# The MLP behind attention in program order, in parts of four and six chunks, with six chunks beside attention instead of seven

## The chip, the cores and the metric

The kernel runs on one core of one Trainium2 chip. The time is the device time of one execution in microseconds (us). The kernel before takes 1400.59 us, the median of three runs (1400.41 to 1401.59). One execution was also taken by the hardware profiler; its span, from the first to the last instruction, is 1397.3 us.

The names of the engines are those of the profile: PE multiplies matrices (TensorE; PEld is its loading of weights), DVE is VectorE, ACT is ScalarE, POOL is GpSimd, and SP issues most of the transfers (DMAs). Each engine works off its own queue in the order in which the instructions stand there. What one engine needs of another it waits for at a semaphore, and all that stands behind the waiting instruction on that engine waits too.

## What is computed

Masked attention over 8 batches of 8 heads (576 positions of 64 numbers), and behind it an MLP with one hidden layer of 2048 over the 4608 rows that attention leaves. q, k, v are float32; `w_in` and `w_out` come as float64.

```python
def attention(q, k, v, tau):                      # (8, 8, 576, 64)
    scores = q @ k.transpose(0, 1, 3, 2) / sqrt(64)
    top = scores.max(-1, keepdims=True)
    scores = where(scores >= top - tau, scores, -1e9)
    a = exp(scores - top)
    return (a / (a.sum(-1, keepdims=True) + 1e-9)) @ v

def mlp(x, w_in, w_out, alpha):                   # x: (4608, 512)
    h = x @ w_in                                  # (512, 2048)
    g = maximum(h, 0) + alpha * minimum(h, 0)
    return g @ w_out                              # (2048, 512)
```

## The kernel before

**Numbers in two parts.** Every operand of the MLP is held as a high and a low part, and a product is three matmuls: high by high, high by low, low by high. The hidden layer is cut into 16 chunks of 128. For one chunk and one group of tokens, layer 1 is 4 blocks of the 512 inputs by 3 products, 12 matmuls into a tile `ph`; layer 2 is 3 matmuls for each 128 tokens, added up over the chunks in a tile `acc`.

**Attention.** Two heads make a pair, and there are 32 pairs, each of nine units (128 queries by one head). The loop over `i` goes through the units in cycles. In each, PE does the scores `s` of one unit and the transposes `t` of another, DVE takes the row maximum (`nmx`, L410), masks (L430) and makes low parts, and ACT does the exponentials and the high parts. The last step of a pair multiplies by v (`av`), turns the reciprocals of the sums (`rp`, L565), fetches them back spread over the partitions (`rb`), and writes a part of x to memory (`fin_mul` L589, `fin_out` L595). The order in which these instructions stand is that in which the code emits them (`manual_schedule`).

**MLP, part 1, beside attention.** The first F1 = 7 chunks are done for groups of G1 = 256 tokens as soon as the x of a group is there, with names that end in "a" (`pha`, `pta`, `ga`, `acca`). There are 18 groups, 0 to 17. `Mlp.cycle` gives out the steps: it has a budget of PE time per cycle (CYCLE) less what attention uses there; a layer 1 step costs 1.31 of it and a layer 2 matmul 0.216. GB buffers hold the `ga`. The sums over the 7 chunks go through `po` to a buffer `part` in memory.

**Decoding.** `Split64` makes the two parts of a float64 weight out of its bits, for one chunk of w_in or w_out (a piece): a load of 512 KB; `size`, two ACT instructions; four steps on DVE and partly POOL (`clamp`, `shift`, `sign`, `power`); `round` on ACT, which makes the high part; `rest`, two steps; and `join` on POOL, which makes the low part and is the last reader of the loaded words. 14 pieces for the 7 chunks are decoded in the first cycles.

**Behind attention.** What is left of part 1 is written by `drain`, outside the manual schedule: there the scheduler of the tool that builds the program orders the instructions by its own estimate of times. The 18 pieces of the other nine chunks are decoded there too, with two buffers `w0` for the loaded words. In this place layer 1's result goes through `hidden`: two DVE instructions (L872, L873), a copy on ACT for the high part and a subtraction on POOL for the low part (both in `split_g`).

**MLP, part 2.** The other nine chunks for nine groups of G2 = 512 tokens, with names that end in "b" (`phb`, `ptb`, `gb`, `accb`): per group nine layer 1 steps, then four blocks of 128 tokens with 27 matmuls each. A block is added to its row of `part` (`pin`, a load) on DVE (`ob`, L903) and stored. The x of a group is loaded at once (`load_x`) and split at once (`split_x`: one ACT copy for `xh`, one POOL subtraction for `xl`).

Of the kernel before, what the change touches and what calls it, by code (L numbers as in the profile page):

```python
# [35 lines left out]
GB = 11  # L36
ENG1 = ('vpp', 'vpp')
ENG2 = ('vvp', 'vvv')
TAIL = 4
# [30 lines left out]
def tile_masked_attention_moe(  # L70
# [31 lines left out]
    class Split64:  # L102
        """float64 bits -> hi + lo in float32r, to 24 bits or better."""
# [105 lines left out]

    def prelu2(t, r, n):  # L210
        nc.gpsimd.tensor_tensor(t[:, :n], t[:, :n], r[:, :n], op=ALU.add)
# [32 lines left out]
    class Turned:  # L244
        """The transposed scores of two heads, in parts, with columns of ones that sum v."""
# [21 lines left out]
    class Pair:  # L267
        """The steps of two heads of one batch; each queues work on one or two engines."""
# [8 lines left out]
        def load(self, what):  # L277
# [11 lines left out]
            if pi == 0:  # L289
                # The first pair's are doubled on the way in, so that its scores start at once.  # L290
# [20 lines left out]
        def prep_first(self, j):  # L311
            """The splits of q and k for one head, before there is other work."""
# [11 lines left out]
        # The two heads' q and k come one above the other. The parts are made so, and then moved:  # L324
        # qst holds the parts of q one above the other, kh and kl each part of k twice.
# [51 lines left out]
        # A unit is (chunk of queries, head), or the tail: the last queries of the  # L377
        # first head above the first queries of the second.
# [63 lines left out]
        def turn_k(self, u):  # L442
            """The keys beyond the four blocks: of both heads at once for a chunk of queries."""
# [13 lines left out]
        def places(self, u):  # L457
            """(PSUM, its place in SBUF by part) for the unit's transposed blocks."""
# [98 lines left out]
        # Divide by the sums; rows that kept no score get the mean of v.  # L557
# [49 lines left out]
    # Where in a pair's nine cycles the work beside the softmax falls.  # L607
# [39 lines left out]
    class Mlp:  # L647
        """The part of the MLP that runs beside attention, a little in each cycle."""
# [15 lines left out]
        def step_l1(self, i):  # L664
# [10 lines left out]

            def act(ph=ph):
                st[fi] = prelu1(mem.mp1, G1, fcs1[fi], n, ph, name, 2)
                prelu2(*st[fi], n)

            def spl():  # L680
                g = mem.mp1.tile([P, 2, G1], F32R, tag="g", name=f"g{name}", bufs=GB)
                split_g(g, st.pop(fi)[0], n, dict(p=nc.gpsimd, v=nc.vector).get(SPG))
                st["g"][fi] = g
# [29 lines left out]
        def cycle(self, i, used, slot):  # L713
            """Work for the tensor engine up to the cycle's length."""
# [12 lines left out]

        def drain(self):
            """What is left when attention is done, in the scheduler's order."""
            for gi, st, fi in list(self.l1):  # L730
                t0, n = groups1[gi]
                if fi is None:
                    pool = (mem.mp1, wp2)[gi % 2]
                    xr = load_x(pool, t0, n, G1, 1)
                    st["x"] = split_x(pool, xr, t0, n, G1, 1)
                else:
                    st["g"][fi] = hidden(mem.mp1, ps_2, G1, fcs1[fi], n, st["x"], f"a{gi}_{fi}", GB)
                if fi == F1 - 1:
                    for o in range(0, n, P):
                        self.l2.extend((0, gi, st, o, fj, ti) for fj in range(F1) for ti in range(3))  # L740
                if not self.l2 or fi != F1 - 1:
                    continue
                while self.l2:
                    _, gj, sj, o, fj, ti = self.l2.popleft()
                    nj = groups1[gj][1]
                    m = min(P, nj - o)
                    if fj == 0 and ti == 0:
                        self.acc = ps_2.tile([P, 512], F32, tag="acc", name=f"acca{gj}_{o}", bufs=4)
                    layer2(self.acc, fcs1[fj], sj["g"][fj], o, m, fj == 0, fj == F1 - 1, (ti,))
                    if fj == F1 - 1 and ti == 2:  # L750
                        po = mem.mp1.tile([P, DM], F32, tag="po", name=f"po{gj}_{o}", bufs=1)
                        nc.scalar.activation(po[:m], self.acc[:m], AF.Copy)
                        nc.sync.dma_start(part[gj][o : o + m, :], po[:m])
                decode_some(4)
            self.l1.clear()
# [14 lines left out]
    # The words of a piece of w_in wait where w_out's parts will be; those of w_out  # L770
    # in the place of its next chunk.
# [6 lines left out]
    for n_, (w, fc, io) in enumerate(pieces):  # L778
        c = DEC0 + DEC * n_ if n_ < F1 else DECO0 + DECO * (n_ - F1)
        if n_:  # L780
            at_cycle(max(-3, c - LD) if io == "i" else c - 3, w.load)
# [62 lines left out]
    for i in sorted({*soon, *later}):  # L844
        for fn, a in soon.get(i, []) + later.get(i, []):
            fn(*a)
# [110 lines left out]
```

## Time and profile before

| | |
|---|---|
| device time, median of 3 runs | 1400.59 us |
| span of the profiled execution | 1397.3 us |
| busy PE / DVE / ACT / POOL | 1339.4 / 975.7 / 820.9 / 762.3 us |
| last row maximum of attention starts | 818.16 us |
| first matmul of part 2 starts | 947.71 us |
| last matmul ends | 1393.5 us |
| mean granted clock of PE | 0.995 |

The time is about 3.3 us above the span. The execution has three stages: attention with part 1 beside it until 818 us; the rest of part 1, with 18 pieces decoded, until 948 us; part 2. Busy time counts matmuls that overlap in the pipeline as one stretch, so a PE that is busy all the time may still have work at less than its best pace. The best pace of a matmul is read from a long row of them without a wait. A line of the trace begins with the start and the length in us; a "x" at its end counts instructions of the row.

### The profile page before, as it was taken

What the parts mean: (1) busy time and instruction counts of PE and PEld (TensorE: products, weight loads), DVE (VectorE), ACT (ScalarE), POOL (GpSimd) and SP (SyncE); (2) the same over time, 40 slices, a digit from 0 to 9 for tenths busy, and PEclk for the clock granted to TensorE, in tenths of its full rate; (3) what the DMA queues carried; (4) which work ended last, traced back from release to release, by engine and by line L of the source; (5) the groups of instructions that cost most, each with busy time, mean ns of one, the idle gap of its engine ahead of it and who ended that gap; (6) DMA issues with size and microseconds to landing.
All of it is one profiled execution on the core that took longest, in us unless ns stands there. A gap on an engine that the chain in (4) does not pass through costs nothing.

```text
span 1397.3 us, 23301 instructions
## 1 busy us (share of the span) xinstructions
PE 1339.4 (96%) x8116; PEld 1181.2 (85%) x8116; DVE 975.7 (70%) x1933; ACT 820.9 (59%) x1843; POOL 762.3 (55%) x821
## 2 busy tenths in 40 slices
PE   5888899999999999999999999888999999999998
PEld 4556789999999999999999998777888888888887
DVE  6999988888888898898888957986323323323332
ACT  7788888888888888888888854453112012111100
POOL 3776676666676666576676557566434124223311
PEclk9999999999999999999999999999999999999999
DMA  8643634545545444454454214433320220111011
GB/s 249 184 127 106 180 105 122 162 116 142 147 117 150 139 134 131 132 154 127 128 160 132 83 57 153 132 109 128 121 74 17 91 91 33 59 61 42 19 61 38
DMA packets 94628, 157.67 MB, mean 113 GB/s; under 512 B 14160, under 2 KB 39024, under 8 KB 94512
## 3 DMA queue, kind: packets, MB, share of 16 engines
q1 hardware_dynamic: 94512, 156.19, 38.4%
q8 instruction: 65, 1.06, 0.3%
q14 instruction: 51, 0.42, 0.1%
HBM read 85.53 MB, written 28.46 MB: 82 GB/s over the span
## 4 chain that ended last, share of the span: by engine, by line
PE 80%; DVE 9%; ACT 4%; DMA 2%; issue 2%; POOL 2%; SPq 0%; DVEq 0%; POOLq 0%; ACTq 0%
PE phb L194 16%; PE accb L224 16%; PE s L395 10%; PE av L542 10%; PE acca L224 9%; PE pha L194 9%; PE t L439 7%; DVE p L430 2%; DVE nmx L410 2%; DMA wri<-in_moe_w_in_dram 1%; PE tk L455 1%; DVE wti L135 1%; POOL wi L152 1%; ACT xb L555 1%; ACT xa L553 1%
## 5 line engine op out<-in xcount | busy, mean ns | idle before, releaser
L410 DVE TENSOR_REDUCE nmx<-s 128x1 f32<-128x576 f32 x288 | 217.0, 753 | 72.6 <-PE s L395 69.5
L215 ACT ACTIVATE gb<-ptb 128x512 fp32r<-128x512 f32 x81 | 50.9, 630 | 337.7 <-DVE ptb L873 337.3
L218 POOL TENSOR_TENSOR gb<-ptb,gb 128x512 fp32r<-128x512 f32 x81 | 104.4, 1290 | 257.0 <-ACT gb L215 256.8
L224 PE MATMUL acca<-wo,ga 128*128 128x512 f32 x756 | 230.7, 419 | 7.2 <-ACT ga L215 4.0
L224 PE MATMUL accb<-wo,gb 128*128 128x512 f32 x972 | 221.9, 389 | 0.0
L224 PEld LDWEIGHTS accb<-wo,gb 128*128 128x128 f32 x972 | 182.4, 188 | 37.9
L430 DVE SCALAR_TENSOR_TENSOR p<-s,thr,p 128x576 f32<-128x576 f32 x256 | 206.6, 807 | 1.3 <-ACT thr L423 0.9
L194 PE MATMUL phb<-xh,wi 128*128 128x512 f32 x648 | 202.9, 392 | 1.1 <-ACT xh L180 1.1
L194 PE MATMUL pha<-xh,wi 128*128 128x256 f32 x1008 | 199.7, 284 | 3.7 <-DVE pta L873 3.4
L418 ACT ACTIVATE p<-s,nmx 128x576 f32<-128x576 f32 x256 | 190.0, 742 | 10.8 <-DVE nmx L410 10.5
L395 PE MATMUL s<-kh,qst 128*128 128x288 f32 x640 | 142.2, 312 | 38.1 <-DVE p L430 23.3
L194 PEld LDWEIGHTS pha<-xh,wi 128*128 128x128 f32 x1008 | 163.8, 190 | 9.9 <-DVE pta L873 4.6
L224 PEld LDWEIGHTS acca<-wo,ga 128*128 128x128 f32 x756 | 132.8, 191 | 28.6 <-ACT ga L215 5.3
L439 PE MATMUL t<-ident,p 128*128 128x128 f32 x1024 | 154.6, 274 | 0.0
L395 PEld LDWEIGHTS s<-kh,qst 128*128 128x128 f32 x640 | 101.4, 193 | 61.5 <-issue 29.4
L903 DVE TENSOR_TENSOR ob<-accb,pin 128x512 f32<-128x512 f32 x36 | 24.2, 689 | 181.9 <-PE accb L224 181.9
L194 PEld LDWEIGHTS phb<-xh,wi 128*128 128x128 f32 x648 | 122.6, 189 | 27.2 <-ACT xh L180 1.5
L194 PE MATMUL pha<-xl,wi 128*128 128x256 f32 x504 | 142.2, 282 | 0.0
L872 DVE TENSOR_SCALAR ptb<-phb,alpha_sb 128x512 f32<-128x512 f32 x81 | 60.7, 751 | 108.5 <-PE phb L194 96.4
L395 PE MATMUL s<-kl,qst 128*128 128x288 f32 x640 | 133.8, 299 | 0.0
L194 PE MATMUL phb<-xl,wi 128*128 128x512 f32 x324 | 127.2, 393 | 3.6 <-POOL xl L182 3.6
L439 PEld LDWEIGHTS t<-ident,p 128*128 128x128 f32 x1024 | 126.5, 141 | 0.1
(117 smaller groups left out, 2772.6 us busy)
## 6 DMA issues: line engine op xcount, KB each, us to landing
kr<-in_k_dram SPq DMA_DIRECT2D x31, 320.0 KB
rb<-rvd SPq DMA_DIRECT2D x64, 144.0 KB
xs<-xa SPq DMA_DIRECT2D x32, 288.0 KB
part<-po SPq DMA_DIRECT2D x36, 256.0 KB
pin<-part SPq DMA_DIRECT2D x36, 256.0 KB
out_dram<-ob SPq DMA_DIRECT2D x36, 256.0 KB
vr<-in_v_dram SPq DMA_DIRECT2D x28, 320.0 KB
qr<-in_q_dram SPq DMA_DIRECT2D x31, 288.0 KB
```

The costliest lines, as they stand in the source:

```text
L194: nc.tensor.matmul(ph[:, :n], w[:, c, :], xx[:, c, :n], start=(c == 0 and ti == 0), stop=(c == NCC - 1 and ti == 2),)
L215: nc.scalar.activation(g[:, 0, :n], t[:, :n], AF.Copy)
L218: nc.gpsimd.tensor_tensor(g[:, 1, :n], t[:, :n], f(g[:, 0, :n]), op=ALU.subtract)
L224: nc.tensor.matmul(acc[:m, :], gg[:, g, o : o + m], w, start=(first and ti == 0), stop=(last and ti == 2))
L395: nc.tensor.matmul(ps[:, h, :288], w, kk[:, a + h * 288 : a + (h + 1) * 288], start=(ki == 0 and i == 0), stop=(ki == 1 and i == n - 1),)
L410: nc.vector.tensor_reduce(self.nmx[:, j : j + 1], self.S[u][0][:, :, :288], axis=AX.XY, op=ALU.max, negate=True)
L418: nc.scalar.activation(pj, ps[:, :, :288], AF.Exp, bias=nmx[:, j : j + 1], scale=1.0)
L430: nc.vector.scalar_tensor_tensor(pj, ps[:, :, :288], thr[:, j : j + 1], pj, op0=ALU.is_ge, op1=ALU.mult, accum_out=self.sm[:, c : c + 1])
L439: nc.tensor.transpose(tb[:, c, :], pt[:, j, j * D + c * P : j * D + (c + 1) * P], ident)
L542: nc.tensor.matmul(pa[:m, :n], w, x, start=(part == 0 and c == 0), stop=(part == z.parts[-1] and c == NKC))
L872: nc.vector.tensor_scalar(t[:, :n], ph[:, :n], 0.0, alpha_sb[:, fc : fc + 1], op0=ALU.min, op1=ALU.mult)
L903: nc.vector.tensor_tensor(ob[:m], acc[:m], pi_[:m], op=ALU.add)
```

## The change

- F1 goes from 7 to 6 and GB from 11 to 10: 12 pieces instead of 14 are decoded early, part 1 has six chunks, and part 2 has ten.
- `drain`, `decode_some` and `hidden` are gone. The loop over `i` now runs on in the manual schedule until part 1 is done, with the whole budget for the MLP once attention is over (`used = 0.0`). A layer 1 step there takes `prelu` (two DVE instructions) and an ACT copy, as `hidden` did.
- Part 2 goes twice over the nine groups: chunks 6 to 9 first, whose sums are added to `part` and written back there, then chunks 10 to 15, whose sums go to the output.
- The eight pieces of chunks 6 to 9 are decoded in the cycles behind attention, one every two cycles (DEC2 = 4, halved); those of chunks 10 to 15 one every five cycles during the first pass of part 2 (a cycle there is a layer 1 step or a block). There are three buffers `w0` instead of two.
- x is fetched for part 2 in four pieces per group (`fetch_x`), each split for itself two cycles later; `pin` is loaded by cycle.

The core of the diff:

```diff
-F1 = 7
+F1 = 6
-GB = 11
+GB = 10
-TAIL = 4
+CLOSE = 9
+DEC2, DEC3 = 4, 5
...
+            alone = i >= total
+
             def act(ph=ph):
+                if alone:
+                    st[fi] = (prelu(mem.mp1, G1, fcs1[fi], n, ph, name, 2),)
+                    return
...
-        def drain(self):
...
+    parts2 = [fcs2[:4], fcs2[4:]]
...
+    def decode_part(part, c0, step):
+        for n_, (io, fc) in enumerate((io, fc) for io in "io" for fc in part):
+            w = Split64(mem.wp2, ("w0", 3), mem.wp2, ("w1", 3), ENG2[(fc + (io == "o")) % 2], *(src_i if io == "i" else src_o)(fc))
+            c = c0 + step * n_ // 2
+            decode_at(c, mem.wp2, w, fc, io, c - 2)
...
+            if i > total + CLOSE and not (mlp.l1 or mlp.l2 or nready < len(groups1)):
+                break
...
+            if i == total + CLOSE:
+                at.close()
+                mem.wp2 = wp2_.enter_context(tc.tile_pool(name="wp2", bufs=1, reuse_waits="tile"))
+                decode_part(parts2[0], i + 3, DEC2)
+                first = fetch_x(mem.wp2, *groups2[0], i + 4, "0_0")
...
+            if i >= total:
+                used = 0.0
...
+        decode_part(parts2[1], i + 3, 2 * DEC3)
+        for num, (p, k) in enumerate(todo):
+            fcs, (t0, n), st = parts2[p], groups2[k], nxt
...
+            for fc in fcs:
+                ph = ps_2.tile([P, 512], F32, tag="ph", name=f"phb{p}{t0}_{fc}", bufs=4)
+                while "x" not in st:
+                    cycle()
+                layer1_into(ph, fc, n, st["x"])
+                cycle()
+                t = prelu(mp2, G2, fc, n, ph, f"b{p}{t0}_{fc}", 2)
...
+                split_g(gg, t, n)
+                g.append(gg)
+            for o, m in blocks:
...
+                for j, fc in enumerate(fcs):
+                    layer2(acc, fc, g[j], o, m, j == 0, j == len(fcs) - 1)
+                cycle()
...
+                dst = out[t0 + o : t0 + o + m, :] if p == len(parts2) - 1 else part[gi][r : r + m, :]
+                nc.sync.dma_start(dst, ob[:m])
```

How the order of the instructions changes is shown at three places. In the names, `wi8` and `wo8` are the two parts of chunk 8's weights, `wti8` and `wri8` their working tile and loaded words, and `ga15_2` is the split hidden layer of group 15, chunk 2; the number behind the last underscore tells buffers apart.

The first is ACT behind attention, where group 14 of the kernel before is done. L123 and L124 are `size`, which waits for the load of its piece, L144 is `round`, L215 the high part of `ga`:

```order
L215 ACTIVATE ga14_1_12391<-pta14_1_12388 128x256
L123 ACTIVATE wti8_12324<-wri8_12322 128x512
L124 ACTIVATE wri8_12322<-wri8_12322 128x512
L215 ACTIVATE ga14_2_12410<-pta14_2_12407 128x256
L123 ACTIVATE wto8_12338<-wro8_12336 128x512
L124 ACTIVATE wro8_12336<-wro8_12336 128x512
L215 ACTIVATE ga14_3_12429<-pta14_3_12426 128x256
L144 ACTIVATE wi8_12331<-wti8_12324 128x512
L215 ACTIVATE ga14_4_12448<-pta14_4_12445 128x256
```

The same engine in the changed kernel, one group later (the lines are now L124, L125, L145 and L222; L720 is `po`):

```order
L145 ACTIVATE wi7_12103<-wti7_12009 128x512
L124 ACTIVATE wti9_12106<-wri9_12060 128x512
L125 ACTIVATE wri9_12060<-wri9_12060 128x512
L808 ACTIVATE xh0_0_12024<-xr0_0_3_12064 128x512
L222 ACTIVATE ga15_0_12139<-pta15_0_12113 128x256
L145 ACTIVATE wi8_12163<-wti8_12057 128x512
L124 ACTIVATE wto6_12166<-wro6_12109 128x512
L125 ACTIVATE wro6_12109<-wro6_12109 128x512
L222 ACTIVATE ga15_1_12171<-pta15_1_12142 128x256
L720 ACTIVATE po14_128_12190<-acca14_128_12069 128x512
L222 ACTIVATE ga15_2_12197<-pta15_2_12174 128x256
```

In both, a `size` stands ahead of copies of `ga`; in the changed kernel the pieces come as four of w_in and then four of w_out, each `size` two cycles behind the last, and parts of x for part 2 stand among them.

The second place is POOL in the changed kernel over the same stretch; L153 is `join`, L225 the low part of `ga`, L150 half of `rest`, L809 a part of `xl`:

```order
L153 TENSOR_TENSOR wi6_12054<-wti6_11959,wri6_11916 128x512
L809 TENSOR_TENSOR xl0_0_12025<-xr0_0_3_12064,xh0_0_12024 128x512
L225 TENSOR_TENSOR ga15_0_12139<-pta15_0_12113,ga15_0_12139 128x256
L153 TENSOR_TENSOR wi7_12103<-wti7_12009,wri7_11962 128x512
L225 TENSOR_TENSOR ga15_1_12171<-pta15_1_12142,ga15_1_12171 128x256
L150 TENSOR_TENSOR wti8_12057<-wti8_12057,wi8_12163 128x512
L225 TENSOR_TENSOR ga15_2_12197<-pta15_2_12174,ga15_2_12197 128x256
L153 TENSOR_TENSOR wi8_12163<-wti8_12057,wri8_12012 128x512
```

Before, the same engine had this there:

```order
L152 TENSOR_TENSOR wo8_12345<-wto8_12338,wro8_12336 128x512
L152 TENSOR_TENSOR wi9_12548<-wti9_12541,wri9_12539 128x512
L218 TENSOR_TENSOR ga15_0_12618<-pta15_0_12615,ga15_0_12618 128x256
L149 TENSOR_TENSOR wto9_12555<-wto9_12555,wo9_12562 128x512
L152 TENSOR_TENSOR wo9_12562<-wto9_12555,wro9_12553 128x512
L218 TENSOR_TENSOR ga15_1_12637<-pta15_1_12634,ga15_1_12637 128x256
```

In the changed kernel one `join` stands behind each one or two `ga`; before, two could follow each other. The load of a piece waits for the `join` that frees its buffer `w0`: that of `wri9` for the `join` of `wi6`, that of `wro6` for that of `wi7`.

The third place is PE in part 2, the first block of the third group and the beginning of its second block. Before, chunk 15's `gb` comes into use late:

```order
L224 MATMUL accb1024_0_14107<-wo13_13053,gb1024_13_14064 128x512 x3
L224 MATMUL accb1024_0_14107<-wo14_13081,gb1024_14_14083 128x512 x2
L224 MATMUL accb1024_128_14140<-wo7_12317,gb1024_7_13950 128x512
L224 MATMUL accb1024_0_14107<-wo14_13081,gb1024_14_14083 128x512
L224 MATMUL accb1024_128_14140<-wo7_12317,gb1024_7_13950 128x512 x2
L224 MATMUL accb1024_128_14140<-wo8_12345,gb1024_8_13969 128x512 x3
L224 MATMUL accb1024_128_14140<-wo9_12562,gb1024_9_13988 128x512
L224 MATMUL accb1024_0_14107<-wo15_13298,gb1024_15_14102 128x512 x2
```

The same group in the changed kernel's first pass, from the last matmul of layer 1 on:

```order
L195 MATMUL phb01024_9_13139<-xh0_2_12929,wi9_12218 128x512
L231 MATMUL accb01024_0_13167<-wo6_12259,gb01024_6_13078 128x512 x3
L231 MATMUL accb01024_0_13167<-wo7_12303,gb01024_7_13103 128x512 x3
L231 MATMUL accb01024_0_13167<-wo8_12359,gb01024_8_13136 128x512 x3
L231 MATMUL accb01024_0_13167<-wo9_12411,gb01024_9_13164 128x512 x3
L231 MATMUL accb01024_128_13188<-wo6_12259,gb01024_6_13078 128x512 x3
```

Before, 24 matmuls of the first block and seven of the second stood ahead of the last chunk's; now nine stand there, and a block is finished before the next begins.

More of the change, by code (lines that the diff above doesn't have):

```diff
@@ L681, in spl @@
                 g = mem.mp1.tile([P, 2, G1], F32R, tag="g", name=f"g{name}", bufs=GB)
-                split_g(g, st.pop(fi)[0], n, dict(p=nc.gpsimd, v=nc.vector).get(SPG))
+                split_g(g, st.pop(fi)[0], n, None if alone else dict(p=nc.gpsimd, v=nc.vector).get(SPG))
                 st["g"][fi] = g
@@ L726, in cycle @@
             return l1
-        def drain(self):
[L730 to L755, printed above, removed]
     mlp = Mlp()
@@ L777, in tile_masked_attention_moe, with decode_at @@
         pieces.append((Split64(stage[0], stage[1], mem, ("g", GB), ENG1[fc % 2], *src_o(fc)), fc, "o"))
[L778 to L781, printed above, removed]
+    def decode_at(c, pool, w, fc, io, load):
+        if load is not None:
+            at_cycle(load, w.load)
         at_cycle(c, w.size)
@@ L803, in tile_masked_attention_moe @@
         p.load("v")
-        for i in range(-3, total + TAIL):
+        i = -4
+        first = None
+        while True:
+            i += 1
+            if i > total + CLOSE and not (mlp.l1 or mlp.l2 or nready < len(groups1)):
+                break
             if i == -1:
@@ L843, in tile_masked_attention_moe @@
                 do(i + 2, "expo")
-    for i in sorted({*soon, *later}):
-        for fn, a in soon.get(i, []) + later.get(i, []):
-            fn(*a)
-    at.close()
-    wp2 = ctx.enter_context(tc.tile_pool(name="wp2", bufs=1, reuse_waits="tile"))
-    ps_2 = ctx.enter_context(tc.tile_pool(name="ps_2", bufs=1, space=PSUM, reuse_waits="tile"))
-    decode = deque((fc, io) for fc in fcs2 for io in "io")
-    def decode_some(n):
-        for _ in range(min(n, len(decode))):
-            fc, io = decode.popleft()
-            w = Split64(wp2, ("w0", 2), wp2, ("w1", 3), ENG2[(fc + (io == "o")) % 2], *(src_i if io == "i" else src_o)(fc))
-            w.load()
-            w.size()
-            w.clamp()
-            w.shift()
-            w.sign()
-            w.power()
-            d = weight(wp2, fc, io)
-            w.round(d[:, 0])
-            w.rest()
-            w.join(d[:, 1])
@@ L878, in tile_masked_attention_moe, with cycle @@
-    while nready < len(groups1):
-        mlp.ready(nready)
-        nready += 1
-    mlp.drain()
-    while decode:
-        decode_some(1)
-    p1.close()
-    mp2 = ctx.enter_context(tc.tile_pool(name="mp2", bufs=1, reuse_waits="tile"))
-    nf = len(fcs2)
-    for t0 in range(0, NT, G2):
-        n = min(G2, NT - t0)
-        pool = (wp2, mp2)[t0 // G2 % 2]
-        xr = load_x(pool, t0, n, G2, 1)
-        x = split_x(pool, xr, t0, n, G2, 1)
-        g = [hidden(mp2, ps_2, G2, fc, n, x, f"b{t0}_{fc}", nf) for fc in fcs2]
-        for o in range(0, n, P):
-            m = min(P, n - o)
-            pi_ = mp2.tile([P, DM], F32, tag="pin", name=f"pin{t0}_{o}", bufs=3)
-            gi, r = divmod(t0 + o, G1)
-            nc.sync.dma_start(pi_[:m], part[gi][r : r + m, :])
-            acc = ps_2.tile([P, 512], F32, tag="acc", name=f"accb{t0}_{o}", bufs=4)
-            for i, fc in enumerate(fcs2):
-                layer2(acc, fc, g[i], o, m, i == 0, i == nf - 1)
-            ob = mp2.tile([P, DM], F32, tag="ob", name=f"ob{t0}_{o}", bufs=3)
-            nc.vector.tensor_tensor(ob[:m], acc[:m], pi_[:m], op=ALU.add)
-            nc.sync.dma_start(out[t0 + o : t0 + o + m, :], ob[:m])
+        def cycle():
+            nonlocal i
+            for fn, a in soon.pop(i, []) + later.pop(i, []):
+                fn(*a)
+            i += 1
@@ new lines, in tile_masked_attention_moe @@
+        while any(c < i for c in [*soon, *later]):
+            c = min([*soon, *later])
+            for fn, a in soon.pop(c, []) + later.pop(c, []):
+                fn(*a)
+        for _ in range(PUTO + 1):
+            cycle()
+        ps.close()
+        ps_2 = ps2_.enter_context(tc.tile_pool(name="ps_2", bufs=1, space=PSUM, reuse_waits="tile"))
+        p1.close()
+        mp2 = mp2_.enter_context(tc.tile_pool(name="mp2", bufs=1, reuse_waits="tile"))
+        todo = [(p, k) for p in range(len(parts2)) for k in range(len(groups2))]
```

73 lines of the change are left out of this document (59 added, 14 removed).

## The prediction

> **What bounds the kernel now.** I read the page first: which engine is busy, and what the chain that ended last is made of.
>
> ```profile
> PE 1339.4 (96%) x8116; PEld 1181.2 (85%) x8116; DVE 975.7 (70%) x1933; ACT 820.9 (59%) x1843; POOL 762.3 (55%) x821
> PE 80%; DVE 9%; ACT 4%; DMA 2%; issue 2%; POOL 2%; SPq 0%; DVEq 0%; POOLq 0%; ACTq 0%
> ```
>
> PE is the bound over the whole, so what counts is PE work and PE waits. But three stages follow each other, and the change takes work out of the first and puts it into the last. The table by stretches shows them: a pair early in attention without MLP or decode, one with five layer 1 steps, two full pairs, the rest of part 1 behind the last row maximum, and part 2. Columns: stretch, length, then busy PE, PEld, DVE, ACT, POOL, the granted clock, DMA.
>
> ```profile
> 138.60:161.20 22.60, 16.93 (x129) 15.80 (x128) 20.93 (x47) 20.51 (x49) 11.40 (x11) 1.00 0.58 155
> 161.20:185.80 24.60, 23.25 (x180) 22.23 (x179) 22.60 (x53) 21.44 (x54) 18.17 (x25) 1.00 0.49 138
> 567.80:593.10 25.30, 25.30 (x184) 24.06 (x183) 22.19 (x50) 21.33 (x52) 14.70 (x20) 1.00 0.46 127
> 593.10:618.60 25.50, 25.42 (x191) 24.35 (x190) 22.61 (x51) 22.54 (x54) 18.82 (x24) 1.00 0.53 146
> 818.20:953.00 134.80, 120.09 (x702) 103.26 (x701) 107.36 (x169) 59.73 (x114) 88.17 (x79) 0.96 0.38 120
> 953.00:1397.30 444.30, 440.53 (x1943) 364.33 (x1942) 145.81 (x208) 69.18 (x96) 147.40 (x94) 1.00 0.19 62
> ```
>
> A full pair has PE busy all along, yet the pair with nothing beside attention still takes 22.60: DVE, 20.93 busy, and the chain of scores, maximum and mask set that. So attention is nearly bound twice, and PE work taken out of it is only partly time saved. Part 2 has no gap at all. The chain there gives PE's pace:
>
> ```profile
> 1001.85 24.48 PE phb L194 x108
> 1026.33 24.48 PE accb L224 x108
> ```
>
> 24.48 / 108 = 0.2267 us for a matmul of 512 columns. The markers that I count from, the first wait of part 2, and two short rows of part 1:
>
> ```profile
> 818.16 0.76 DVE L410 TENSOR_REDUCE nmx<-s 128x1 f32<-128x576 f32 x1 [0.58 <-PE s L395]
> 830.49 0.27 PE L565 MATMUL rp<-ident,rv 128*9 128x128 f32 x1
> 942.99 4.68 POOL xl L182
> 947.71 7.36 PE phb L194 x21
> 825.87 1.42 PE pha L194 x12
> 830.76 6.38 PE acca L224 x28
> ```
>
> From `rp` to the first `phb` are 117.2 us. By the order of instructions PE has 372 matmuls of 256 columns and 220 of 512 there. The short rows give 1.42 / 12 = 0.118 and 6.38 / 28 = 0.228; I take 0.119 and 0.2285: 44.3 + 50.3 = 94.6. So the old end of part 1 has 22.6 us in which PE waits or runs slower. This is what a better order could win at most.
>
> **The change, stage by stage.** *Attention.* Counted in the order of PE, part 1's work ahead of the last scores is 1104 matmuls of 256 and 504 of 512 before, 960 and 441 now: 246.6 us against 215.0, 31.6 less. What of it is saved I take from the pairs above. Nothing beside attention against a full pair: (25.3 - 22.6) / 9.7 = 0.28, where 9.7 is the MLP work of a full pair (246.6 over the 25.5 pairs that have it). Five layer 1 steps, 5 x 12 x 0.119 = 7.1 us: (25.3 - 24.6) / (9.7 - 7.1) = 0.27; with the 25.5 of the other full pair 0.35. I take 0.30: **-9.5 us**. The ends are 0.2 (-6) and all of it (-31.6), if PE alone set the pace.
>
> Two fewer pieces are decoded early. The four pairs ahead of the pair above, with 12 of the 14 pieces:
>
> ```profile
> 34.30:138.60 104.30, 91.08 (x500) 60.95 (x499) 99.50 (x186) 84.90 (x196) 72.30 (x61) 1.00 0.49 140
> ```
>
> (104.30 - 4 x 22.60) / 12 = 1.16 us each, so **-2.3 us** (0 to three times that, -7). The last row maximum moves from 818.2 to 806.4. From there to `rp` were 12.3 us. The order has 12 matmuls of 256 fewer in it and 18 of 512 more: 2.7 us, so 15.0.
>
> *From `rp` to part 2.* PE's work there is 312 x 0.119 + 180 x 0.2285 = 78.2 us. The question is what it waits for. Two things at once: the low part of group 13's last `ga` stands on POOL behind `fin_mul`, which waits for `rb`, as it did before:
>
> ```profile
> 837.05 1.21 POOL L589 TENSOR_TENSOR xa<-xa,rb 128x576 f32<-128x576 f32 x1 [2.88 <-DMA rb<-rvd]
> ```
>
> That starts 6.56 after `rp`. With its own 1.21 and `ga`'s 0.87 the low part is there at 8.6, and PE has work until 6.7; then the `xl` of group 14 (2.65, below) keeps PE again. Together **3.8**.
>
> Then the decode. What a loop of it is made of, from the chain and from the groups between 818 and 953 us (busy us and mean ns of one, then idle time ahead of it):
>
> ```profile
> 857.35 3.87 DMA wro<-in_moe_w_out_dram
> 868.02 4.42 DMA wri<-in_moe_w_in_dram
> 872.47 0.67 ACT wti L123
> 877.55 1.32 POOL wi L152
> 878.88 4.56 DMA wri<-in_moe_w_in_dram
> L215 ACT ACTIVATE ga<-pta 128x256 fp32r<-128x256 f32 x30 | 12.1, 411 | 18.2 <-DVE pta L873 18.2
> L124 ACT ACTIVATE wri<-wri 128x512 f32<-128x512 uint32 x9 | 6.0, 667 | 0.0
> L180 ACT ACTIVATE xh<-xr 128x1024 fp32r<-128x1024 f32 x4 | 4.2, 1051 | 0.0
> L218 POOL TENSOR_TENSOR ga<-pta,ga 128x256 fp32r<-128x256 f32 x34 | 29.4, 873 | 10.2 <-ACT ga L215 9.7
> L152 POOL TENSOR_TENSOR wi<-wti,wri 128x512 fp32r<-128x512 f32 x8 | 11.4, 1424 | 9.8 <-DVE wti L149 9.7
> L182 POOL TENSOR_TENSOR xl<-xr,xh 128x1024 fp32r<-128x1024 f32 x4 | 10.6, 2647 | 3.9 <-ACT xh L180 3.9
> ```
>
> In the chain, a load follows the join that frees its buffer without a pause (877.55 + 1.32, then 878.88). In the order of the changed kernel the load of piece n+3 waits for the join of piece n; its `size` stands on ACT ahead of the next `ga`; and the next join stands on POOL behind that `ga`. So joins follow each other at: load 4.4, `size` 0.67 + 0.67, a part of `xh` or `po` (0.5), `ga` 0.41, its low part 0.87, join 1.42: 8.9, and about 0.1 for each of six hand-overs, 9.5. Where a second `ga` or a `rest` (L149's kind, 1.4) lies between, it is more. Going row by row through the four such loops, I get 9.8, 10.7, 9.3 and 11.1, 40.9 us in all. PE needs each `ga` too, and has 13.2 us of work there: **27.7 lost**, in waits of 6.7, 7.3 and 7.4 and smaller ones. The ends: nothing, if the loads come ahead of this or the joins find room; and 35, with the slowest load (4.6) and the joins at 1.7. I take the middle, since each piece is a measured row. Before, joins could follow each other and the scheduler moved PE's steps about: a loop of 10.86 (868.02 to 878.88) carried two pieces.
>
> Groups 16 and 17 each begin with `xh` and `xl` behind the last layer 1 step of the group before, 1.05 + 2.65 and the `ga` ahead, some 5.6 to 6.9 us against 4.8 of work between: **4.2** for both (0 to 6). In all 78.2 + 3.8 + 27.7 + 4.2 = 113.9.
>
> *The clock.* Behind the last wait of before (3.6 us, the idle time of the group below), 21 matmuls took 7.36 where 21 x 0.2267 = 4.76: 2.6 lost, at a mean granted clock of 0.89 over that stretch.
>
> ```profile
> L194 PE MATMUL phb<-xl,wi 128*128 128x512 f32 x324 | 127.2, 393 | 3.6 <-POOL xl L182 3.6
> 947.70:970.00 22.30, 22.29 (x88) 18.13 (x89) 17.26 (x28) 7.02 (x12) 13.11 (x10) 0.89 0.52 172
> ```
>
> The three long waits could each cost that, 7.8. But between them PE is not what sets the pace; I take **2.6**, for the last. The Trainium skill, "TensorE: Matmul & The Clock Gate" (Part 1: The HAM clock gate), says that PE's clock falls to half after an idle window of about 3.4 us and comes back after as long a busy one. The trace agrees as far as its one wait of that length goes. By that rule alone each long wait would cost about 1.7 us (an estimate, half of 3.4), 5.1 in all.
>
> *Part 2.* The matmuls are 9 x 10 x 24 = 2160 at 0.2267: **489.7 us**, against 440.6 for nine chunks. That is 49 us of a chunk that moves here from the two stages before it. A new wait comes with the four-chunk groups. The time from a layer 1 result to the low part of `gb`:
>
> ```profile
> 1121.64 0.75 DVE L872 TENSOR_SCALAR ptb<-phb,alpha_sb 128x512 f32<-128x512 f32 x1 [1.24 <-PE phb L194]
> 1122.43 0.69 DVE L873 SCALAR_TENSOR_TENSOR ptb<-phb,ptb 128x512 f32<-128x512 f32 x1
> 1123.24 0.63 ACT L215 ACTIVATE gb<-ptb 128x512 fp32r<-128x512 f32 x1 [2.09 <-DVE ptb L873]
> 1123.94 1.29 POOL L218 TENSOR_TENSOR gb<-ptb,gb 128x512 fp32r<-128x512 f32 x1 [1.43 <-ACT gb L215]
> 1124.09 11.27 PE L224 MATMUL accb<-wo,gb 128*128 128x512 f32 x49
> 1124.36 0.75 DVE L872 TENSOR_SCALAR ptb<-phb,alpha_sb 128x512 f32<-128x512 f32 x1 [1.24 <-PE phb L194]
> ```
>
> The last chunk's DVE work starts 0.27 after layer 2 began (1124.36 - 1124.09), and from there to the end of the low part are 1125.23 - 1121.64 = 3.59: 3.86, and a hand-over. With nine chunks the matmul that needs it is the 27th, at 26 x 0.2267 = 5.9; with four it is the 12th, at 2.49. So 1.4 us per group, **12.9** for nine. With six it is at 3.85, just in time: 2 for nine. Where a join or `rest` of the spread pieces stands ahead of `gb` on POOL, one or two groups lose 1.1 more: 2. Sum **17** (10 if the hand-overs are short, 25 if POOL is late in most groups). The additions and stores of the first pass are DVE and SP work, and DVE is a third busy there; their cover is PE.
>
> *End.* From the last matmul on:
>
> ```profile
> 1379.93 13.61 PE accb L224 x60
> 1393.57 0.69 DVE ob L903
> ```
>
> 1397.3 - 1393.5 = 3.8, unchanged.
>
> *Sum*, against the span of 1397.3: 806.4 + 15.0 + 113.9 + 2.6 + 489.7 + 17 + 3.8 = 1448.4. The runs stand 3.3 above the span: **1451.7 us, 51 slower**. In short, 31.3 us of PE work leave attention, where they are worth 9.5, and come back behind it at full price, with 55 us of waits where 23 were.
>
> **Rivals.**
> 1. *The decode loop is hidden*: loads or joins come earlier than I follow them. For it: the DMA engines were 0.38 busy in that stage before, and POOL has room. Against: the order is fixed, and the loop is only rows in series. Then -27.7 - 2.6: 1421.
> 2. *Attention follows PE*, so all 31.6 are saved. For: PE 25.30 of 25.30 busy. Against: the pair of 24.60, which had 2.6 us less work and saved 0.7 to 0.9. Then 22.1 less: 1430.
> 3. *Faster: the program order keeps PE fed.* If every `ga`, `x` and `gb` is ready when PE comes to it, the waits behind attention (35.7 + 2.6 + 17 = 55.3) are gone: 1396.4, and with rival 2 as well 1374. It decides from where these waits fall under 4 us, or under 26 together with rival 2. For: busy DVE, ACT and POOL sums are below PE's in each stage. Against: a fixed order lets PE do nothing else while it waits for the last chunk of four, and before, the scheduler itself left 22.6.
> 4. *Worse*: clock losses in all three long waits (+5.2) and POOL late in most groups (+8): 1465.
> That the change does not do what it says is excluded for its order, which is fixed when the program is built.
>
> **How the numbers follow.** The forecast 0.57; rival 1 0.13; rival 2 0.10; rival 3 0.09 (of it 0.07 faster and 0.02 near the old time); rival 4 0.11. The range 1416 to 1468 takes in the forecast with its bounds, rivals 1, 2 and 4, and leaves out rival 3 and the tails. A measurement here tells 0.2%, 2.8 us, from no change; rivals 1 and 2 together (1399) give the same a little more: faster 0.07, same 0.03, slower 0.90.
>
> **What would show it.** Right: the last row maximum near 806; between `rp` and the first `phb` about 114 us, with three PE waits near 7 us on `ga` and loads of `wri` and `wro` in the chain; in the first pass a wait of 1.4 us at the last chunk's `gb` in each group, none in the second. Wrong: a full pair shorter by over 0.6 us; `size` waiting for no load; part 2 at 490 us. If part 2 has waits elsewhere, it will be at `xl` or `pin`.

## The result

The changed kernel takes 1476.86 us (median of four runs, 1470.92 to 1478.55) against 1401.07 us (1400.41 to 1401.59): a ratio of 1.0538, with a 95% interval of 1.0514 to 1.0563. It is slower, as forecast, but by 76 us and not by 51, and the time lies above the range given (1416 to 1468). Its runs also lie further apart than those before: 7.6 us against 1.2. The profile is of the slowest of the four, 1478.55 us at a span of 1476.7; the runs stand 1.8 us above the span of the same execution, and not the 3.3 that the forecast added from two different ones. One run of all those below, of e1, was in a slower state (1537.60 us at a granted clock of 0.843) and is left out of the times.

The page's busy times and the chain by engine, of the changed kernel:

```profile
PE 1367.6 (93%) x8008; PEld 1186.3 (80%) x8008; DVE 999.8 (68%) x1967; ACT 841.3 (57%) x1897; POOL 788.7 (53%) x846
PE 73%; DVE 10%; POOL 6%; ACT 4%; issue 4%; DMA 1%; SPq 0%; POOLq 0%; ACTq 0%; DVEq 0%
```

PE's share fell from 96% to 93%, and POOL's in the chain rose from 2% to 6%. The mean granted clock fell from 0.995 to 0.979. Set against the sum of the forecast, stage by stage (us):

| | forecast | measured |
|---|---|---|
| last row maximum (818.2 before) | 806.4 | 825.0 |
| from there to `rp` | 15.0 | 15.1 |
| from `rp` to the first `phb` | 116.5 | 113.1 |
| part 2 up to the last matmul | 506.7 | 519.8 |
| end | 3.8 | 3.7 |
| span | 1448.4 | 1476.7 |

The forecast's sum is 28.3 us short: 18.6 in attention, where it saw a gain, and 13.1 in part 2, less 3.4 between `rp` and part 2. (The marker of 947.71 us for part 2 before is the end of a wait; three of its matmuls had run at 941.5 already. The sum of the forecast does not use it.)

Attention in the table by stretches, with the columns as above: the pair without MLP work, a full pair, the pair behind it, and an earlier one of the same make; then the rest of part 1, and the two passes of part 2.

```profile
134.10:156.70 22.60, 16.93 (x130) 15.81 (x128) 20.89 (x46) 20.51 (x49) 11.39 (x11) 1.00 0.59 156
675.00:700.30 25.30, 25.30 (x184) 24.00 (x183) 22.11 (x49) 21.20 (x52) 14.63 (x19) 1.00 0.45 127
700.30:726.10 25.80, 23.31 (x173) 21.91 (x172) 22.13 (x50) 22.17 (x53) 16.98 (x21) 1.00 0.52 144
593.90:622.50 28.60, 26.11 (x173) 24.46 (x172) 22.20 (x50) 22.23 (x53) 16.97 (x21) 0.88 0.46 130
840.10:953.20 113.10, 86.67 (x495) 72.99 (x492) 61.05 (x97) 36.49 (x71) 58.14 (x53) 0.92 0.33 106
953.20:1176.50 223.30, 206.98 (x864) 165.11 (x865) 118.79 (x173) 63.05 (x108) 119.16 (x90) 0.97 0.47 149
1176.50:1473.00 296.50, 296.14 (x1297) 242.37 (x1295) 102.79 (x144) 51.72 (x86) 109.74 (x86) 1.00 0.29 91
```

The pair without MLP work starts at 134.1 instead of 138.6: with fewer early pieces, 4.5 us are gained (2.3 forecast). The full pair is the same as before, 184 matmuls in 25.30 us. In the last third of attention all the work that is gone is missing from every other pair (by the counts, 36 matmuls of layer 1 and 12 of layer 2 instead of 48 and 18), and those did not get shorter: 25.80, where PE now stands idle for 2.5 us. And in some of them the clock is lower: 28.60 us at 0.88 for the same 173 matmuls. That one more closely:

```profile
593.90:597.00 3.10, 3.10 (x27) 3.05 (x25) 2.80 (x6) 2.71 (x6) 2.76 (x2) 1.00 0.24 56
597.00:600.00 3.00, 1.55 (x10) 1.00 (x8) 2.96 (x8) 2.91 (x8) 1.86 (x3) 1.00 0.91 262
600.00:603.00 3.00, 1.96 (x9) 1.98 (x10) 1.91 (x5) 2.77 (x5) 1.45 (x1) 0.56 0.96 283
603.00:606.00 3.00, 3.00 (x11) 2.52 (x11) 1.93 (x5) 1.58 (x4) 2.31 (x2) 0.50 0.41 87
606.00:609.00 3.00, 3.00 (x21) 3.00 (x21) 0.38 (x1) 0.76 (x2) 0.00 (x0) 0.80 0.99 295
609.00:612.00 3.00, 3.00 (x23) 2.66 (x22) 2.53 (x6) 2.70 (x7) 0.39 (x2) 1.00 0.16 54
```

Two cycles with little or no MLP work leave PE busy for 3.5 of 6 us; in the second of them the clock goes to half and stays there for 6.8 us (what the rows of 0.56, 0.50 and 0.80 lack, 3 x (0.44 + 0.50 + 0.20) = 3.4 us, is half of that; so it begins at 600.4), and a cycle full of matmuls falls into that time (eleven in 3 us, where the first and the last row, at 1.00, have 27 and 23). The table of waits of that pair shows that no single wait was long:

```profile
PE s L402 <- DVE p L437: 2.5, 2, 1.6
```

The columns are the us in total, the number and the longest: two waits, of 0.9 us (up to 598.2) and 1.6 us (599.5 to 601.0).

### The profile page after: what moved, and what is told of

It reads as the page before. It is cut to its first block, busy times and chain, and to the rows that moved or that the text cites. A ratio compares the mean times of both kernels' runs of the same rounds, so it can differ in the third digit from the quotient of the medians.

```text
span 1476.7 us, 23646 instructions
## 1 busy us (share of the span) xinstructions
PE 1367.6 (93%) x8008; PEld 1186.3 (80%) x8008; DVE 999.8 (68%) x1967; ACT 841.3 (57%) x1897; POOL 788.7 (53%) x846
## 3 DMA queue, kind: packets, MB, share of 16 engines
q8 instruction: 64, 1.05, 0.3%
## 4 chain that ended last, share of the span: by engine, by line
PE 73%; DVE 10%; POOL 6%; ACT 4%; issue 4%; DMA 1%; SPq 0%; POOLq 0%; ACTq 0%; DVEq 0%
PE accb L231 15%; PE phb L195 12%; PE av L549 11%; PE s L402 10%; PE acca L231 8%; PE pha L195 8%; PE t L446 7%; POOL gb L225 3%; DVE p L437 2%; DVE nmx L417 2%; POOL xl L809 1%; PE tk L462 1%; DVE eo L502 1%; ACT eo L498 1%; POOL wi L153 1%
## 5 line engine op out<-in xcount | busy, mean ns | idle before, releaser
L231 PE MATMUL accb<-wo,gb 128*128 128x512 f32 x1080 | 261.0, 399 | 16.7 <-POOL gb L225 14.3
L231 PEld LDWEIGHTS accb<-wo,gb 128*128 128x128 f32 x1080 | 204.8, 192 | 69.9 <-POOL gb L225 22.2
L222 ACT ACTIVATE gb<-ptb 128x512 fp32r<-128x512 f32 x90 | 56.9, 632 | 355.2 <-DVE ptb L214 355.2
L225 POOL TENSOR_TENSOR gb<-ptb,gb 128x512 fp32r<-128x512 f32 x90 | 118.2, 1314 | 260.1 <-ACT gb L222 259.5
L195 PE MATMUL phb<-xh,wi 128*128 128x512 f32 x720 | 224.7, 389 | 0.7 <-ACT po L720 0.7
L231 PE MATMUL acca<-wo,ga 128*128 128x512 f32 x648 | 202.9, 430 | 15.7 <-ACT ga L222 9.7
L195 PE MATMUL pha<-xh,wi 128*128 128x256 f32 x864 | 174.1, 286 | 6.4 <-DVE pta L214 4.4
L936 DVE TENSOR_TENSOR ob<-accb,pin 128x512 f32<-128x512 f32 x72 | 49.8, 692 | 186.7 <-PE accb L231 184.7
L195 PEld LDWEIGHTS pha<-xh,wi 128*128 128x128 f32 x864 | 141.0, 190 | 12.3 <-DVE pta L214 5.1
L231 PEld LDWEIGHTS acca<-wo,ga 128*128 128x128 f32 x648 | 118.9, 199 | 35.0 <-ACT ga L222 11.2
L195 PE MATMUL pha<-xl,wi 128*128 128x256 f32 x432 | 122.5, 283 | 3.9 <-POOL xl L183 3.9
```

The lines of the kernel that those rows point to most:

```text
L195: nc.tensor.matmul(ph[:, :n], w[:, c, :], xx[:, c, :n], start=(c == 0 and ti == 0), stop=(c == NCC - 1 and ti == 2),)
L222: nc.scalar.activation(g[:, 0, :n], t[:, :n], AF.Copy)
L225: nc.gpsimd.tensor_tensor(g[:, 1, :n], t[:, :n], f(g[:, 0, :n]), op=ALU.subtract)
L231: nc.tensor.matmul(acc[:m, :], gg[:, g, o : o + m], w, start=(first and ti == 0), stop=(last and ti == 2))
L936: nc.vector.tensor_tensor(ob[:m], acc[:m], pins[o][:m], op=ALU.add)
```

## The experiments

All ratios are to the kernel before on the same chip: e1 to e4, e5 to e8 and e9 to e11 ran on three chips, on which it took 1401.15, 1400.42 and 1399.69 us. Differences to the changed kernel are to its 1476.86 us, which was measured once and whose runs differ by 7.6 us, so they are good to a few us. The last row maximum, `rp`, the first `phb` and the end are read from each trace; "part 2" in this section goes from the first `phb` to the end of the span (523.5 us in the changed kernel).

**e1 and e2: the two halves of the change.** e1 is the kernel before with only this:

```diff
-F1 = 7
+F1 = 6
-GB = 11
+GB = 10
```

> The kernel before with six chunks beside attention (F1 = 6, GB = 10) and nothing else changed: part 2 in one pass of ten chunks, drain as it was. Theory (attention itself got longer with less MLP work, since its empty cycles let PE idle and the clock fall): the last row maximum comes near 825 us as in the changed kernel, not near 806; the whole 1440 to 1450 us. Rival (attention got longer by something in the new code): last row maximum 803 to 813, the whole 1420 to 1430.

1443.18 us (median of three, 1442.81 to 1447.28), ratio 1.0298 (1.0278 to 1.0319). The last row maximum is at 821.7, and its pairs 7 to 10 (counted from 0) take 28.47, 25.27, 26.91 and 24.81 us, as those of the changed kernel do (28.43, 25.28, 26.85, 24.82). So attention gets longer by taking a chunk away, without any of the new code. (The 3.3 us to the changed kernel's 825.0 are two later pairs, which take 28.52 and 27.30 us there and 26.98 and 25.71 here.)

e2 is the changed kernel with seven chunks:

```diff
-F1 = 6
+F1 = 7
-GB = 10
+GB = 11
```

> The changed kernel with seven chunks beside attention (F1 = 7, GB = 11), so parts of four and five behind it. Theory: last row maximum at 818 as before, from rp to the first phb about 125 us (a seventh chunk adds 13 us of work to 113), part 2 about 470 (440.6 and 28 of waits and lost clock): 1430 to 1440 us. Rival (the new tail changes attention too): last row maximum past 823.

1445.84 us, ratio 1.0323 (1.0305 to 1.0342), 6 above the expectation. The last row maximum is at 819.1, so the new tail leaves attention alone. From `rp` to `phb` it takes 132.9 (125 expected), part 2 475.4 (470 expected). The halves cost about 42 and 45 us by themselves, and both together 76.

**e3: more work for PE.** In the changed kernel, the 14 cycles of attention that have neither MLP work nor `av` get matmuls that nobody reads (`mlp.given` counts the layer 2 matmuls of a cycle):

```diff
+                self.given += 1
...
+            elif 54 <= i < total and i not in busy and not mlp.given:
+                warm = ps_m.tile([P, 512], F32, tag="pm", name=f"warm{i}")
+                for _ in range(8):
+                    nc.tensor.matmul(warm[:, :256], wi[0][:, 0, :P], wi[0][:, 0, :256], start=True, stop=True)
```

> The changed kernel with 8 matmuls of 256 columns, whose result nobody reads, in each of the 14 cycles of attention that have neither MLP work nor av: 112 matmuls, 13 us of added PE work. Theory (clock): the granted clock in pairs 7, 9, 15, 19, 23 and 25 comes back to 1.00 and attention ends 8 to 12 us sooner, the last row maximum at 813 to 817, although PE has more to do. Rival (those pairs are long because of a chain on ACT and DVE, not of the clock): no gain, attention 0 to 13 us later.

1465.86 us (1464.91 to 1466.58), 11 less than the changed kernel with 112 matmuls more, and the runs lie within 1.7 us. The last row maximum is at 814.8. The same two pairs as above, of the same make (the earlier and the later one):

```profile
588.20:613.90 25.70, 24.17 (x180) 22.83 (x179) 22.09 (x49) 22.12 (x53) 16.92 (x20) 1.00 0.50 145
690.20:715.90 25.70, 24.17 (x180) 22.82 (x179) 22.07 (x49) 22.09 (x53) 16.89 (x20) 1.00 0.51 145
```

28.60 became 25.70, with the clock at 1.00. The 25.8 of the undisturbed pair stayed, though PE does more in it: there its work costs nothing. So some 10 us of attention's 18.6 (825.0 less 814.8) were lost clock. The other 8.4 are not, or hardly: from pair 8 on the clock in e3 is at 1.00 throughout.

**e6: the work spread thinner.** The only edit to the changed kernel:

```diff
-CYCLE = 2.6
+CYCLE = 2.5
```

> The changed kernel with CYCLE 2.5 instead of 2.6, so that the MLP work of six chunks is spread thinner and no cycle of attention runs dry; a little more of it is left behind attention. Theory of the empty cycles: clock 1.00 through attention, no pair over 26 us, last row maximum 806 to 814. If attention also saves time by less MLP work per pair, as forecast (0.3 us for each us), it is at 800 to 806. Rival (empty cycles don't matter): 820 or later. The whole 1460 to 1472 us, since the work left behind grows by 10 to 15 us.

1455.38 us, 21.5 less than the changed kernel. The last row maximum is at 805.6, where the forecast had 806.4. The whole is better than the 1460 to 1472 expected: from `rp` to `phb` are 113.8 us as before the edit, and by the counts the same 312 matmuls of layer 1 and 180 of layer 2 are left for it. A pair of each kind:

```profile
659.70:684.30 24.60, 24.60 (x186) 23.51 (x185) 22.52 (x51) 21.61 (x53) 16.43 (x22) 1.00 0.46 130
684.30:709.40 25.10, 23.94 (x171) 22.21 (x170) 21.66 (x49) 21.76 (x52) 15.23 (x17) 1.00 0.54 149
```

With the budget of 2.6, six chunks fill every cycle as seven did until the work runs out, and then leave whole cycles empty. With 2.5, the fuller pair is shorter by 0.7 us, though it has two matmuls more: 48 of layer 1 and 14 of layer 2 where 36 and 24 were, which by the prediction's 0.119 and 0.2285 us are 8.9 us instead of 9.8. From pair 8 on no pair takes more than 25.1; pair 7, where layer 2 begins, takes 27.59 with its clock down (27.12 before). Spread like this, the work that is gone does save about what the two early pairs of the forecast said; taken out of some cycles almost entirely it saves nothing. But 0.30 is a mean of two kinds of pair: the fuller one saves 0.7 us for 0.9 us of work less, the other about 0.3 for 1.8.

**e11: the copy of x.** In the empty cycle the copy of `xh` (1.05 us) stands on ACT ahead of the high part of the turned scores. To see whether it keeps the pair long, the kernel of e3 does it behind:

```diff
-                at_cycle(i + XO, lambda: st.update(x=split_x(mem.mp1, st["xr"], t0, n, G1, 1)))
+                last.setdefault(i + XO, []).append(lambda: st.update(x=split_x(mem.mp1, st["xr"], t0, n, G1, 1)))
...
             do(i, "hi_k")
             do(i, "hi")
+            for fn in last.pop(i, []):
+                fn()
```

> Kernel e3 (work in the empty cycles) with the split of part 1's x put behind the copies of the turned scores on ACT instead of ahead of them. Theory (in an empty cycle the 1.05 us copy of xh holds up the high part on ACT, then DVE's low part and the next row maximum): the pairs with an empty cycle from 25.7 to 25.0 to 25.3, the last row maximum from 814.9 to 806 to 811, the whole 4 to 8 us less than e3. Rival (a pair's length does not hang on that copy): within 1 us of 814.9.

No gain: 1465.89 us, last row maximum 815.1, as the rival said. The empty cycle fell from 3.15 to 2.38 us, and the next one rose from 3.20 to 3.93. This theory fell. What holds the pair with an empty cycle at 25.7 was not found.

**e4: the next chunk ahead of layer 2.** In part 2, for each group (`hidden` is here layer 1 of one chunk with its `prelu` and split, `fetch` the call of `fetch_x`; the part of the edit that only moves code into these two is left out):

```diff
...
+            for j in range(1, len(fcs)):
+                hidden(num, j)
+            if num + 1 < len(todo):
+                hidden(num + 1, 0)
+            fetch(num + 2)
...
```

> The changed kernel with part 2 written so that layer 1 of the next group's first chunk (2.72 us) stands ahead of layer 2 of this group, and x of the group after is fetched a half group sooner. Theory (a block waits for the last chunk's gb, and where it waits twice the clock falls): part 2 from 523.5 us to 495 to 503, the whole 20 to 28 us less than the changed kernel. Rival (POOL is what part 2 runs at in its first pass): 5 us or less.

1457.44 us, 19.4 less; part 2 502.0 instead of 523.5. The waits of part 2 in the changed kernel:

```profile
PE accb L231 <- POOL gb L225: 14.3, 13, 2.9
PE accb L231 <- ACT gb L222: 2.4, 7, 0.3
PE phb L195 <- ACT po L720: 0.7, 1, 0.7
```

and in e4:

```profile
PE phb L195 <- POOL xl L809: 3.1, 3, 1.7
PE phb L195 <- ACT po L720: 0.7, 1, 0.7
PE phb L195 <- ACT xh L808: 0.6, 1, 0.6
```

The waits on `gb` are gone. They came to 16.7 us, and 21.5 were won. New waits on x cost 3.7, so 13.0 of the 21.5 are waits. The clock accounts for no more than 3.4: in part 2 half of two stretches of 6.8 us was not granted in the changed kernel, and half of one such stretch in e4 (969 to 976 us). A further 2 to 3 are an estimate: a matmul by itself takes 0.39 us in the trace and one in a long row 0.2267, and some 20 starts behind a wait are gone, for four new ones. The rest was not traced. In the changed kernel the worst group of the first pass had these stretches behind its last layer 1 matmul:

```profile
1011.20:1016.00 4.80, 2.99 (x12) 1.84 (x11) 2.37 (x4) 1.53 (x3) 4.80 (x4) 1.00 0.21 55
1016.00:1020.00 4.00, 2.45 (x6) 1.97 (x7) 1.29 (x2) 0.00 (x0) 2.73 (x3) 0.60 0.74 204
1020.00:1024.00 4.00, 4.00 (x12) 3.11 (x11) 0.49 (x1) 2.30 (x4) 1.29 (x1) 0.55 0.74 231
1024.00:1029.00 5.00, 5.00 (x24) 4.10 (x23) 2.42 (x5) 0.00 (x0) 0.62 (x1) 1.00 0.62 191
```

and on POOL, whose 4.80 of 4.80 stands in the first of them, this (start, us, instruction):

```profile
1009.64 1.29 POOL L150 TENSOR_TENSOR wti<-wti,wi 128x512 f32<-128x512 f32 x1
1010.89 1.48 POOL L809 TENSOR_TENSOR xl<-xr,xh 128x512 fp32r<-128x512 f32 x1
1012.34 1.28 POOL L225 TENSOR_TENSOR gb<-ptb,gb 128x512 fp32r<-128x512 f32 x1
1013.59 1.47 POOL L153 TENSOR_TENSOR wi<-wti,wri 128x512 fp32r<-128x512 f32 x1
1015.02 1.26 POOL L809 TENSOR_TENSOR xl<-xr,xh 128x512 fp32r<-128x512 f32 x1
```

Half of a piece's `rest`, a part of `xl`, the second last `gb`, a `join`, another `xl`, and only then the `gb` that PE waits for. That group's layer 2 took 17.7 us where 48 x 0.2267 are 10.9.

**e5: words of their own.** The loads of the eight pieces behind attention go into the places of weights that are needed later, so that none waits for a `join`; the working tile gets four buffers instead of three:

```diff
-            w = Split64(mem.wp2, ("w0", 3), mem.wp2, ("w1", 3), ENG2[(fc + (io == "o")) % 2], *(src_i if io == "i" else src_o)(fc))
+            raw = ("w0", 3)
+            if part is parts2[0]:
+                raw = [(f"w{a}{b}", 1) for a in "io" for b in parts2[1]][n_]
+            w = Split64(mem.wp2, raw, mem.wp2, ("w1", 4), ENG2[(fc + (io == "o")) % 2], *(src_i if io == "i" else src_o)(fc))
```

> The changed kernel, where the loaded words of each of the eight pieces decoded behind attention have a place of their own (that of a weight of chunks 10 to 15, which is needed later) and the working tile has four buffers instead of three: no load waits for a join. Theory (the loop from join to load to size to ga to join sets the pace there): from rp to the first phb from 113 us to 84 to 92, no PE wait of 4 us or more on ga or po, the whole 20 to 28 us less than the changed kernel. Rival (DVE's and POOL's own work sets the pace there): 105 us or more from rp to phb.

1462.29 us, 14.6 less (20 to 28 expected). From `rp` to `phb` are 101.6 us: between the theory's 84 to 92 and the rival's 105. The loop was there, and the edit takes 11.5 us off this stage, net of what sets the pace next; which of its two parts does it was not tried apart. What shows next is DVE (stretch of 30 us, third of the busy times):

```profile
880.00:910.00 30.00, 21.93 (x121) 17.44 (x120) 29.76 (x43) 12.92 (x24) 20.90 (x16) 0.89 0.15 45
```

DVE is busy for 29.76 of 30.00 us with decoding and `prelu`, and the clock is at 0.89 again.

**e7, e8, e9 and e10: the repairs together.** e8 is the changed kernel with the edits of e3, e4 and e5; e7 is seven chunks with those of e4 and e5 (and two `w0` buffers instead of three); e9 is e7 with a piece every three cycles (`DEC2` 4 to 6); e10 is six chunks with the budget of 2.5, the edits of e4 and e5, and `DEC2` 5.

> The changed kernel with all three repairs: work in the empty cycles, the next group's first chunk ahead of layer 2, words with places of their own. If the three causes are separate and add up (11, 19 and 20 to 28 us): 1414 to 1428 us. If they are the same lost clock counted more than once: 1432 or more.

1436.89 us, in the rival's range; the theory's range counted 20 to 28 us for e5, which gave 14.6. It is 40.0 less than the changed kernel, of 45 by the single runs. By stage they nearly add up: 10.2 in attention, 11.5 from `rp` to `phb` and 21.5 in part 2 are 43.2, and e8 has 10.1, 9.3 and 22.1, 41.4 in all.

> Seven chunks beside attention with the new tail (parts of four and five), and both repairs: the next group's first chunk ahead of layer 2, and words with places of their own (working tile four buffers, w0 two). Theory (the new tail loses by the decode loop and the gb waits alone): last row maximum 819, from rp to phb 97 to 108 instead of 133, part 2 450 to 462 instead of 475: 1390 to 1412 us, near or under the kernel before. Rival (the new tail loses by something that neither repair touches): 1425 us or more.

1408.38 us, ratio 1.0062 (1.0039 to 1.0084). The whole and part 2 (452.9) are as expected, but from `rp` to `phb` are 117.8, not 97 to 108.

> Kernel e7 (seven chunks, both repairs) with the eight pieces behind attention one every three cycles instead of two (DEC2 = 6). In e7 DVE was busy 9.9 of 10 us for 30 us there and PE's clock was 0.8. Theory (with the loop gone, DVE's decode work in too short a stretch keeps PE): from rp to phb 117.8 falls to 104 to 112, the whole 1396 to 1404 us. Rival (what is left there is the order of xl and ga on POOL): within 3 us of e7's 1408.

1405.56 us, ratio 1.0050 (1.0037 to 1.0063). From `rp` to `phb` are 113.5, at a clock of 0.92:

```profile
837.80:951.30 113.50, 102.97 (x588) 90.78 (x586) 68.04 (x107) 38.68 (x76) 64.00 (x58) 0.92 0.30 103
```

The stage and the time both miss the theory's 104 to 112 and 1396 to 1404, and the time is within 3 us of e7's, as the rival said; by the ratios to the kernel before, e9 cannot be told from e7. The largest waits there are on `xl` of part 1's groups (7.9 us in four), which is the rival's place too. The edit did not settle what holds that stage.

> The changed kernel (six chunks) with the budget of 2.5, the next group's first chunk ahead of layer 2, words with places of their own, and a piece every two and a half cycles (DEC2 = 5). If the repairs add up (21, 19, 15 and some 5): 1415 to 1423 us. If six chunks behind a good tail were as good as seven: 1400 to 1408.

1418.73 us, ratio 1.0138 (1.0123 to 1.0154), as expected of separate repairs. So with six chunks the program order ends 19 us behind the old kernel on the same chip, and with seven 6 us. None of these kernels beats it.

## Why the prediction was wrong

**Attention: the step that failed.** The prediction took 31.6 us of PE work out and said "I take 0.30: -9.5 us", with ends of -6 and -31.6. (It gives this work once as 31.3; its counts make 31.5.) What came was +11.3: the last row maximum moved from 818.2 to 825.0, +6.8, although 4.5 of decoding were gained. The rate came from two pairs whose cycles had no MLP work or at most one layer 1 step each; it was then laid on pairs in which the budget deals out the work. e6 shows that the rate is right in the mean for work that is spread (805.6), and the changed kernel that it is not for work dealt out at the old rate until there is none. From pair 8 on, where e3 and e6 have the clock at 1.00, e6 is 22.5 us shorter than the changed kernel and e3 8.9: so 8.9 of the 22.5 are the clock, and 13.6 come of how the work is dealt out. Why a pair with almost empty cycles takes 25.7 even at full clock stays open; e11 only moved the time to the next cycle. That a saving could have the wrong sign was outside the bounds, because the clock was weighed only behind attention.

**The clock: a term too small.** The prediction allowed 2.6 us for it, for one wait among three of 6.7 to 7.4. Mean clock 0.979 over 1476.7 us is 31 us of full clock not granted, and 0.995 over 1397.3 is 7: some 24 more, not all of it lost, since PE also waits in those stretches. The spread of the runs goes with it: the four runs had 0.978 and 0.979 (1478.5 us), 0.981 (1475.2) and 0.984 (1470.9). It did not take waits of 3.6 us: at 600.4 us the clock fell 0.9 us into the second of two waits of 0.9 and 1.6 us. The trace before had shown as much in attention, where one wait of 2.06 us was followed by a stretch at half clock, and that pair (185.8 to 212.9 us) took 27.1 us where full ones take 25.3:

```profile
193.41 0.51 PE L395 MATMUL s<-kh,qst 128*128 128x288 f32 x2 [2.06 <-DVE p L430]
195.00:198.00 3.00, 3.00 (x15) 3.00 (x15) 1.51 (x4) 2.10 (x6) 2.95 (x2) 0.50 0.58 133
```

Even in the prediction's own wait, 944.2 to 947.7 us, the clock was down from 945.8 on (0.72 over 944 to 948). The Trainium skill ("TensorE: Matmul & The Clock Gate", Part 1: The HAM clock gate) says that the window in which PE's activity is weighed runs freely, so that the point at which the clock changes varies from run to run. That agrees with the two pairs above, where the same two waits of together 2.5 us led to 0.88 in one pair and 1.00 in the other. Its rule of an idle window of about 3.4 us does not agree with a fall 0.9 us into a wait, if idle is meant to the letter; the measurement decides.

**From `rp` to part 2: the size was right, its parts less so.** 113.1 against 116.5. Idle PE time there is 26.4 (113.1 less 86.67 busy) where the prediction had 35.7 of waits. The clock of 0.92 withheld another 9 (0.08 x 113.1), where it had 2.6; that is about what busy time exceeds the 78.2 of work by. So a wait term too large and a clock term too small nearly cancel, which is luck. The waits stand where they were put:

```profile
PE acca L231 <- ACT ga L222: 9.7, 2, 4.9
PE pha L195 <- DVE pta L214: 4.4, 2, 2.9
PE acca L231 <- ACT po L720: 4.0, 1, 4.0
PE pha L195 <- POOL xl L183: 3.9, 4, 1.2
```

`ga`, `pta` and `po` behind the decode loop, and `xl` at the groups' heads, but none near 7 us. The loop itself is in the chain, with each load at the end of a join:

```profile
874.45 1.46 POOL wi L153
875.92 4.03 DMA wri<-in_moe_w_in_dram
884.00 1.43 POOL wi L153
885.45 3.26 DMA wro<-in_moe_w_out_dram
910.75 1.77 POOL wo L153
912.54 4.05 DMA wro<-in_moe_w_out_dram
```

From the first of these joins to the last are four loops, 36.6 us (875.9 to 912.5) where 40.9 were forecast. Rival 1 (the loop hidden, -30.3) was priced too high as well: e5 took the loop away and won 11.5 us in this stage.

**Part 2: the place was right, the size was not.** 17 us above the matmuls' best pace were forecast and 30.1 came (519.8 less 489.7). The second pass had next to none (296.50 for 1296 matmuls, 293.8 by 0.2267), the first 27.4 (223.30 for 864, 195.9). 1.4 us in each four-chunk group was about right for five groups, whose layer 2 took 12.4 to 12.7 us instead of 10.9. In the other four, where pieces and parts of x stood ahead of `gb` on POOL, 3.0 and 3.1 us were lost at full clock and 5.9 and 6.8 where the clock fell too (1016 to 1024 and 1068 to 1076 us), and not 2.5; the prediction had priced pieces there, but no parts of x. The upper end of 25 was still too low.

**The rest** came as worked out: the way from the last row maximum to `rp`, the matmuls of part 2, the end. Rival 3 (the program order keeps PE fed) did not come, and the experiments do not settle what it would give: e10 comes within 19 us of the old kernel, but still takes 100.2 us from `rp` to `phb` where the work is 78.2.

## What to carry to other kernels

Before work is taken off an engine that shares a loop, ask which cycles it leaves: a budget that deals out work until there is none made empty cycles here, and only thinner full ones were shorter. An empty stretch on PE can also cost the clock of the next, so a schedule with gaps should be read in the granted clock by stretches of a few us, not in the longest wait. When a pipeline's chunk count per group is cut, work out the way from the last result to its first use, and count on the engine in between what else stands ahead of it.

## What the hardware showed

The clock fell to 0.50 at 600.4 us, 0.9 us into the second of two waits of 0.9 and 1.6 us; in a pair with the same waits (700 to 726 us) it did not fall. It stayed there for 6.8 us, and so it did in the two stretches of part 2 (1016 to 1024 us: twice 4 x (0.40 + 0.45) us; 1068 to 1076: twice 4 x (0.50 + 0.35)). 112 matmuls that nobody reads, 13 us of PE work, made the kernel 11 us faster and its spread 1.7 us instead of 7.6.
